# A TensorE-bound fused kernel on one core: a new plan with spare time at hand-overs, two groups normalised by VectorE from PSUM, and a new order of TensorE's steps

## The chip, the cores and the metric

The kernel runs on one core of one Trainium2 chip. The metric is the device time of one execution in microseconds. Before the change it took 386.89 us (median of three runs, 386.45 to 387.34).

## The reference

Two stages follow each other. The first is attention inside chunks of 64 rows, for 8 batches, 8 heads, 576 rows and a head size of 64. Its result, with the heads side by side, is the input x (8 x 576 x 512) of the second: four experts, each a causal attention with one head of 64, mixed by the softmax of the two largest of four gate logits.

```python
# stage 1, per batch, head and chunk of 64
scores = q_c @ k_c.T / sqrt(64); attn = softmax(scores); x = attn @ v_c
# stage 2, per batch and expert e
logits = x @ w_gate                     # two largest of four are kept
q, k, v = x @ wq[e], x @ wk[e], x @ wv[e]
a = softmax(causal(q @ k.T / sqrt(64)))
out += weight_e * (a @ v @ wo[e])       # weight_e: softmax over the two kept, else 0
```

## The kernel before, in words

Rows are cut into 36 groups of 128 (4608 rows in all). A unit is one or two groups; the first four units hold one group each. TensorE does its work in 374 named steps, and the letters name what a step does:

- `as` (line 532): score products of a unit's chunks, 64x64 matmuls in a quarter of the array. `as0.1` is half of `as0`; only units 0 and 1 (`FAST`) are split so.
- `at` (line 600): transposes of the normalised chunk weights, on half of the array's rows. `av` (line 621): their products with v, in quarters again; they give x.
- `m` and `v` (line 483): the projections of x to queries and keys (`m`, 52 steps of 12 matmuls) and to values and gate logits (`v`, 36 steps), on the full array. x and the weights are held as a high and a low part, and three products are added up. The first of these steps are split in two (`m1`, `m1.1`), so that the part that needs only high parts can go early.
- `s` (line 760): causal scores of an expert pair, six pieces for each of 16 pairs, on half of the rows. `st` (line 834): transposes of the finished weights. `o` (line 867): weights times values, on half of the columns, 16 steps. `w` (line 902): the output projection, 36 steps on the full array.

So a step has one of four forms of the array: full, rows (half of the rows), quarters, cols (half of the columns).

Between these, VectorE takes row maxima and subtracts them (lines 550, 562), sums exponentials (570, 575, 577), takes reciprocals (579), splits off low parts (644, 682, 684, 886), adds the causal mask and takes the minimum (772), and copies a part of the transposes and outputs (605, 814, 916). ScalarE takes exponentials (568, 573, 779) and copies from PSUM (464, 512, 608, 642, 677, 848, 882, 913). GpSimd multiplies the chunk weights by the reciprocals (586), makes the low parts of the weights (468), computes the gates (710 to 734) and scales the expert weights (803). Group 1 alone has its exponentials in PSUM (`FROM_PSUM`) and is normalised by VectorE (582), in two instructions.

There are eight PSUM banks, and they go round: a step takes the banks that were given back first. Which bank a step writes, and so whose copy it has to wait for, is fixed when the program is built.

The order is set in three ways. `ORDER` is a list, written out, of TensorE's steps. Every other queue (VectorE, ScalarE, GpSimd, SP with its transfers) is filled by a planner, `Plan.emit`, that runs through the program with a table of durations and delays and puts next, on each engine, the ready operation with the smallest key; the key is worked out backwards from the step of TensorE that needs the result (`rank`), and moved by tables (`LATER` by kind, `MOVED` by single operation, `EARLY` and `LOADS` for the first ones). `lat` is the delay that the planner puts between an operation and the one that uses its result. So the tables move instructions, while no duration in them is the chip's. Dummy matmuls (line 944, `FILLS`) stand at four places of the start.

## Time and profile before

| what | value |
|---|---|
| median of three runs | 386.89 us |
| the profiled execution | 386.81 us |
| its span, first to last instruction | 385.1 us |
| mean granted TensorE clock | 0.998 |
| TensorE matmuls busy | 376.4 us, 98% of the span |
| VectorE, ScalarE, GpSimd busy | 71%, 70%, 44% |
| moved by DMA | 40.76 MB, mean 106 GB/s |

The profiled execution took 1.7 us more than its span. In a timeline row the first two figures are the start and the length in us; then follow engine, source line, operation, destination and sources with shapes, and the count of merged instructions; in square brackets stands the idle time of the engine ahead of it and what ended that. A row of waits gives the waiting engine with its line, what it waited for, the total in us, the number of times and the longest. A matmul counts as busy until its modelled end, and the next one starts before that end, so busy time is not the sum of useful work. PEld is the loading of the stationary operand, which runs ahead of its matmul.

### The profile page before, as it was taken

The numbers are of one execution on the slowest core, as the hardware profiler recorded it, in microseconds if no ns is written. First come the engines' busy times: TensorE is split into PE (matmuls) and PEld (weight loads), VectorE is DVE, ScalarE is ACT, GpSimd is POOL, SyncE is SP. The second block draws the span as 40 slices with busy tenths as digits, with TensorE's granted clock in tenths as the row PEclk, the third lists the DMA queues.
The fourth block names the chain that finished last, engine by engine and source line by source line (L and its number), as shares of the span: only waits on it lengthen the run. The fifth ranks groups of instructions, "written<-read, shape, count | busy, mean of one in ns | idle before, by whom it ended". The sixth has DMA issues, their size and how long they took to land.

```text
span 385.1 us, 14193 instructions
## 1 busy us (share of the span) xinstructions
PE 376.4 (98%) x5604; PEld 331.7 (86%) x5605; DVE 272.4 (71%) x955; ACT 270.6 (70%) x899; POOL 170.4 (44%) x337
## 2 busy tenths in 40 slices
PE   7899999999999999999999999999999999999996
PEld 5699999978899979987999879988899998796764
DVE  3768989998984866968897375468739584557821
ACT  4565879797583995589935698349974597689551
POOL 7643167916354008950943002960651108624800
PEclk9999999999999999999999999999999999999999
DMA  7965726047450026420651200111101000000314
GB/s 270 383 213 180 219 86 220 5 129 243 162 184 2 4 91 233 174 83 3 228 183 59 84 0 30 48 63 47 69 34 53 0 24 35 2 30 0 139 56 163
DMA packets 22098, 40.76 MB, mean 106 GB/s; under 512 B 2448, under 2 KB 2704, under 8 KB 22032
## 3 DMA queue, kind: packets, MB, share of 16 engines
q1 hardware_dynamic: 21744, 39.47, 30.0%
q8 instruction: 44, 0.72, 0.8%
q10 hardware_dynamic: 288, 0.39, 0.3%
q14 instruction: 22, 0.18, 0.1%
HBM read 30.42 MB, written 9.44 MB: 104 GB/s over the span
## 4 chain that ended last, share of the span: by engine, by line
PE 88%; DVE 5%; ACT 4%; DMA 1%; issue 0%; SPq 0%; ACTq 0%; DVEq 0%
PE bank L483 39%; PE bank L902 12%; PE bank L760 10%; PE bank L867 10%; PE bank L834 6%; PE bank L621 4%; PE bank L532 4%; PE bank L600 2%; DMA qs<-in_qt_dram 1%; ACT at L779 1%; DVE mx L575 1%; DVE mx L550 1%; ACT aT L848 1%; DVE e L562 1%; ACT xh L642 1%; DVE aT L814 1%
## 5 line engine op out<-in xcount | busy, mean ns | idle before, releaser
L803 POOL TENSOR_SCALAR at<-at,st,gate 128x320 f32<-128x320 f32 (+4 forms) x160 | 94.5, 605 | 29.4 <-ACT at L779 16.2
L779 ACT ACTIVATE at<-at,st 128x320 f32<-128x320 f32 (+4 forms) x160 | 90.3, 598 | 0.9 <-DVE st L772 0.9
L483 PE MATMUL bank<-xh,wqk_hi 128*128 128x384 f32 (+1 forms) x208 | 66.1, 327 | 0.1
L483 PE MATMUL bank<-xl,wqk_hi 128*128 128x384 f32 (+1 forms) x208 | 65.1, 323 | 0.0
L483 PE MATMUL bank<-xh,wqk_lo 128*128 128x384 f32 (+1 forms) x208 | 65.1, 323 | 0.0
L848 ACT ACTIVATE aT<-bank 128x128 f32<-128x128 f32 (+2 forms) x256 | 57.6, 406 | 8.2 <-PE bank L834 8.1
L772 DVE CUSTOM_DVE_ANT_0 at<-bank,mask 64x64 f32<-64x64 f32 (+4 forms) x160 | 59.3, 423 | 3.4 <-PE bank L760 1.8
L586 POOL TENSOR_TENSOR e<-e,mx 128x1024 f32<-128x1024 f32 (+1 forms) x21 | 34.1, 1629 | 53.1 <-DVE mx L579 52.4
L867 PE MATMUL bank<-aT,vv 128*64 128x448 f32 (+4 forms) x384 | 45.0, 390 | 0.0
L867 PEld LDWEIGHTS bank<-aT,vv 128*64 128x64 f32 x384 | 24.4, 137 | 20.8 <-issue 15.4
L710 POOL TENSOR_TENSOR gs<-vv,gs 128x20 f32<-128x20 f32 x8 | 2.4, 299 | 89.5 <-DVE gs L704 89.5
L814 DVE STREAM_TRANSPOSE aT<-at 32x96 f32<-32x96 f32 x128 | 34.4, 269 | 9.7 <-POOL at L803 5.9
L483 PE MATMUL bank<-wvg_hi,xh 128*128 128x260 f32 x144 | 40.5, 288 | 0.0
L483 PE MATMUL bank<-wvg_lo,xh 128*128 128x260 f32 x144 | 39.8, 283 | 0.0
L483 PE MATMUL bank<-wvg_hi,xl 128*128 128x260 f32 x144 | 39.5, 281 | 0.0
L483 PEld LDWEIGHTS bank<-xh,wqk_hi 128*128 128x128 f32 x208 | 38.4, 188 | 1.0 <-ACT xh L642 0.2
L483 PEld LDWEIGHTS bank<-xl,wqk_hi 128*128 128x128 f32 x208 | 38.4, 189 | 0.2
L483 PEld LDWEIGHTS bank<-xh,wqk_lo 128*128 128x128 f32 x208 | 38.4, 188 | 0.0
L760 PE MATMUL bank<-kh,qh 64*128 64x288 f32 (+4 forms) x192 | 38.3, 338 | 0.0
L779 ACT ACTIVATION_READ_ACCUMULATOR at<-at,st 128x1 f32 (+1 forms) x160 | 37.6, 236 | 0.0
L760 PE MATMUL bank<-kl,qh 64*128 64x288 f32 (+4 forms) x192 | 34.3, 296 | 0.0
L760 PE MATMUL bank<-kh,ql 64*128 64x288 f32 (+4 forms) x192 | 32.8, 291 | 0.0
(96 smaller groups left out, 846.0 us busy)
## 6 DMA issues: line engine op xcount, KB each, us to landing
ks<-in_kt_dram SPq DMA_DIRECT2D x36, 256.0 KB, 4.6
vs<-in_vt_dram SPq DMA_DIRECT2D x36, 256.0 KB, 4.5
qs<-in_qt_dram SPq DMA_DIRECT2D x35, 256.0 KB, 4.7
out_dram<-y SPq DMA_DIRECT2D x35, 256.0 KB, 2.0
at<-in_wqk_dram SPq DMA_DIRECT2D x4, 256.0 KB, 5.7
at<-in_wvg_dram SPq DMA_DIRECT2D x2, 260.0 KB, 5.3
at<-in_wo_dram SPq DMA_DIRECT2D x2, 256.0 KB, 5.3
qs<-in_qt_dram ACTq DMA_DIRECT2D x1, 256.0 KB, 3.7
```

The lines of the kernel that those rows point to most:

```text
L483: pe.matmul(bk.t[:, :n_], a, x, start=(n == 0), stop=(n == 3 * KT - 1))
L532: pe.matmul(bq[s].t[cs, c0:c0 + 64], qs[n].t[own, hp, cs], ks[n].t[own, hp, cs], start=(n == 0 and hp == 0), stop=True, skip_group_check=True)
L586: od = [add("Pool", 0.14 + 0.87 * G, lambda: pool.tensor_tensor(e.t[:, al], e.t[:, al], mx.t[:, 3, al, 0:1].to_broadcast([128, 2 * nh, 64] ...
L760: pe.matmul(bks[s].t[:m, :w], q[own, cs], k[own, z0 + ks.start:z0 + ks.stop], start=(x == 0), stop=(x == 2))
L772: dve.tensor_tensor_reduce(out=a.t[:r, o_ + ks.start:o_ + ks.stop], in0=bk.t[:r, :w], in1=mask[:r, m0:m0 + w], scale=1.0, scalar=first, op ...
L779: act.activation(af, af, AF.Exp, scale=-1.0, bias=st.t[:r, 0, i, 0:1], accum_out=st.t[:r, 1, i, 0:1])
L803: pool.tensor_scalar(af, af, st.t[:r, 2, i, 0:1], gt.t[:r, i, e:e + 1], op0=OP.mult, op1=OP.mult)
L814: dve.transpose(dst, src)
L834: pe.transpose(bks[r].t[:, 64 * n:64 * n + 64], a.t[own, c0:c0 + 128], ident[own, own])
L848: act.activation(dst, bks[r].t[:, n:n + 64 * m].rearrange("p (j c) -> p j c", j=m), AF.Copy)
L867: pe.matmul(bk.t[64 * s:64 * s + 64, c0 - h0:h1 - h0], vs.t[:, j, 64 * (2 * pair + s):64 * (2 * pair + s) + 64], ts[s].t[:, place(s, j, c0 ...
L902: pe.matmul(bk.t, up[:, k, u0:u0 + 128], wp[:, k, :], start=(n == 0), stop=(n == 5))
```

## The change

It edits the planner's rules and its tables; the arithmetic changes at one place, group 0.

```diff
-FROM_PSUM = (1,)
+FROM_PSUM = (0, 1)
...
+SPARE = 0.07
+PAUSES = ((3.8, 0.4), (9.0, 1.3))
...
     def lat(self, a, b):
         if b.eng == "dma":
             return 1.9
+        if a.eng == "dma":
+            return 1.1 if b.eng == "ACT" else 0.8
         if a.eng == "SP":
             return 0.1
-        if a.eng == "dma":
-            return 0.9 if b.eng == "ACT" else 0.6
-        return self.LAT.get((a.eng, b.eng), 0.21)
+        return self.LAT.get((a.eng, b.eng), 0.21) + (SPARE if a.eng != b.eng else 0.0)
...
-        state = {"form": "full", "at": 192, "cross": 0.0, "block": 0.0, "pause": 1.2}
+        state = {"form": "full", "at": 192, "cross": 0.0, "block": 0.0}
...
+        pauses = list(PAUSES)
...
-                if eng == "dma" and now > 7.0 and state["pause"]:
-                    dur += state["pause"]
-                    state["pause"] = 0.0
+                if eng == "dma" and pauses and now > pauses[0][0]:
+                    dur += pauses.pop(0)[1]
...
-as0.1 as0 as1 as1.1 at0 at1 av0 av1 as2 m0 v0 v0.1 m2 as3 m1 v1 m1.1 m0.1 v1.1 m2.1 m3 m3.1 at2 at3 as4 av2 av3 as5
+as0.1 as0 as1.1 as1 at0 at1 av0 av1 as3 as2 m1 m0 m1.1 m3 m2 m3.1 m2.1 v1 m0.1 v0 as4 at3 at2 s0.1 s0 as5 av3 av2
...
-COLD = 6.5
+COLD = 8.0
...
-LOADS = [(x[:2], int(x[2:])) for x in "lq0 lq1 lv0 lv1 lw4 lw5 lw0 lw2 lw1 lw3 lq2 lv2 lq3 lv3 lq4 lv4".split()]
+LOADS = [(x[:2], int(x[2:])) for x in "lq0 lw4 lq1 lw5 lw0 lv0 lv1 lw2 lw1 lw3 lq2 lq3 lv2 lv3 lq4 lv4".split()]
```

`SPARE` and `PAUSES` are no instructions: they widen the delays with which the planner reckons, between two different engines by 0.07, and put two pauses into its picture of the transfers. `LATER`, `MOVED` and `EARLY` are replaced as well (`ap0@Pool` is gone from `EARLY`, `ap0` and `ap0.1` of VectorE are in it). All steps of `ORDER` are the same, in another sequence. Group 0's product with the reciprocals goes from one instruction of GpSimd (line 586) to two of VectorE (line 582 before, 586 after); its exponentials now go to PSUM. Lines of the changed kernel stand four further down.

Three places, as they stand in the program. First VectorE's queue from the second half of group 0's maxima on. `mx_84` belongs to group 0, `mx_85` to group 1. Before:

```order
L562 TENSOR_TENSOR e_81<-bank_62,mx_84 128x256 [waits DVE_49]
L570 TENSOR_REDUCE mx_84<-e_81 128x4 [waits Activation_49]
L550 TENSOR_REDUCE mx_85<-bank_64 128x4 [waits PE_49]
L570 TENSOR_REDUCE mx_84<-e_81 128x4 [waits Activation_49]
...
L579 RECIPROCAL mx_84<-mx_84 128x8 [waits DVE_49]
...
L579 RECIPROCAL mx_85<-mx_85 128x8 [waits DVE_49]
L582 TENSOR_TENSOR e_82<-bank_63,mx_85 128x256 [waits DVE_49]
L582 TENSOR_TENSOR e_82<-bank_64,mx_85 128x256
L605 COPY e_81<-bank_66 128x256 [waits PE_49]
L605 COPY e_82<-bank_68 128x256 [waits PE_49]
```

After:

```order
L566 TENSOR_TENSOR e_81<-bank_62,mx_84 128x256 [waits DVE_49]
L574 TENSOR_REDUCE mx_84<-bank_61 128x4 [waits Activation_49]
L554 TENSOR_REDUCE mx_85<-bank_63 128x4 [waits PE_49]
L554 TENSOR_REDUCE mx_85<-bank_64 128x4 [waits PE_49]
...
L583 RECIPROCAL mx_84<-mx_84 128x8 [waits DVE_49]
L586 TENSOR_TENSOR e_81<-bank_62,mx_84 128x256 [waits DVE_49]
L586 TENSOR_TENSOR e_81<-bank_61,mx_84 128x256
L574 TENSOR_REDUCE mx_85<-bank_64 128x4 [waits Activation_49]
...
L586 TENSOR_TENSOR e_82<-bank_63,mx_85 128x256 [waits DVE_49]
L609 COPY e_81<-bank_66 128x256 [waits PE_49]
L586 TENSOR_TENSOR e_82<-bank_64,mx_85 128x256
```

Group 0's two products now stand ahead of the last sum of group 1, and the copy of group 0's transposes stands between the two products of group 1.

Second, SP's queue of transfers at the start (q of group 0 goes through ScalarE's queue in both). Before:

```order
L425 DMA ks_73<-in_kt_dram 128x512
L461 DMA at_100<-in_wqk_dram 128x512
L425 DMA ks_74<-in_kt_dram 128x512
L426 DMA qs_70<-in_qt_dram 128x512
L461 DMA at_101<-in_wvg_dram 128x520 x2
L429 DMA vs_77<-in_vt_dram 128x512
```

After:

```order
L429 DMA ks_73<-in_kt_dram 128x512
L429 DMA ks_74<-in_kt_dram 128x512
L430 DMA qs_70<-in_qt_dram 128x512
L433 DMA vs_77<-in_vt_dram 128x512
L465 DMA at_100<-in_wqk_dram 128x512
L429 DMA ks_75<-in_kt_dram 128x512
```

k and q of group 1 (`ks_74`, `qs_70`) stand one place further up, ahead of the first piece of weights, and both pieces of the value weights (`wvg`) come later.

Third, TensorE's queue where the chunk weights of units 2 and 3 are transposed. A rank of eight transposes goes in turn to two banks; one row for each bank is shown. Before (`at2`, `at3`, `as4`, `av2`):

```order
L600 MATMUL bank_68<-ident,e_83 128x64 [waits Activation_49,Pool_49]
L600 MATMUL bank_63<-ident,e_83 128x64 [waits DVE_49]
...
L600 MATMUL bank_62<-ident,e_81 128x64 [waits Pool_49]
L600 MATMUL bank_64<-ident,e_81 128x64 [waits DVE_49]
...
L532 MATMUL bank_67<-ks_73,qs_69 64x64 [waits DMAHW3_49,DMAHW2_49,DVE_49]
...
L621 MATMUL bank_61<-e_83,vs_79 64x64 [waits DMAHW6_49,DVE_49,Activation_49]
```

After (`at3`, `at2`, `s0.1`):

```order
L604 MATMUL bank_62<-ident,e_81 128x64 [waits Pool_49]
L604 MATMUL bank_65<-ident,e_81 128x64 [waits DVE_49]
...
L604 MATMUL bank_63<-ident,e_83 128x64 [waits Pool_49]
L604 MATMUL bank_61<-ident,e_83 128x64 [waits DVE_49]
...
L764 MATMUL bank_62<-kh_94,qh_90 128x192 [waits Activation_49]
L764 MATMUL bank_65<-kh_94,qh_90 128x192 [waits Activation_49]
```

The two banks of `at3` are now written again by `s0.1`, with only the eight transposes of `at2` in between.

More of the change, by code (lines that the diff above doesn't have):

```diff
@@ L298 @@
-av17 av18 o8 o9 m42 v28 at19 s11.5 st43 s11 s11.2 s11.1 st42 st40 w19 v29 v27 v30 w20 m43 m41 av19 av20 as21 m40 m45
-m44 m47 m46 st44 st46 s12.2 st45 s12.4 st47 s12.5 st41 s12.1 s13.4 s12 at21 s13.5 s13.1 s13.2 s13.3 s12.3 s13 av21
-w21 v31 m49 m51 w18 m50 m48 o11 o10 st50 st51 st55 st49 v32 v34 v33 w23 v35 st48 s14.4 st52 st53 s14.1 s14 s15.4 s15
-st54 s14.5 s15.2 s15.1 s15.5 s14.3 s14.2 s15.3 o13 o12 w24 w25 w22 w26 st60 st58 st61 st63 w28 w27 w29 st62 st59
-st56 st57 o15 o14 w30 w33 w34 w35 w31 w32
+as0.1 as0 as1.1 as1 at0 at1 av0 av1 as3 as2 m1 m0 m1.1 m3 m2 m3.1 m2.1 v1 m0.1 v0 as4 at3 at2 s0.1 s0 as5 av3 av2
@@ new lines @@
+v0.1 v1.1 as6 m7 v2 m5 v3 s1 at4 at5 s1.2 s1.3 m6 as8 av5 av4 as7 m4 m10 m8 v4 m11 m9 s0.3 at6 s1.4 s0.2 s0.4 av6
+s1.1 at7 s1.5 s0.5 as10 av7 as12 v8 m12 v5 v7 m13 m14 st6 st5 at8 st1 st4 m15 v6 st0 st7 s3.1 s3.3 st2 st3 s2.2 s2.5
+s2.4 as9 av8 o1 o0 s3 s2 s2.3 at12 at10 s3.4 s3.5 s2.1 s3.2 at9 v10 m18 v9 v11 m19 as11 av9 as13 av10 m16 m17 m20
+m22 v12 m23 st8 st9 st12 m21 st10 st11 s4.4 st14 s4.1 at11 s4 st13 s4.5 s5.1 at13 s4.2 st15 s5.4 s5.5 s4.3 s5.2 s5.3
+av11 as16 o3 o2 w1 v13 v17 w0 w2 m24 v16 w4 v14 w6 st17 s5 st16 av12 av13 as15 as14 w7 m25 v15 m27 m26 w5 st20 st19
@@ new lines @@
+st21 w3 w8 st22 s7.4 st18 s7.1 at16 s6 st23 s7.2 at14 s6.2 at15 s6.4 s6.1 s6.5 s7.5 s7.3 s6.3 o4 o5 s7 st27 st25
+av14 as18 av15 w11 m29 v21 v19 m33 m28 w9 st24 st28 m30 m31 v20 v18 m32 m35 st30 s8.2 st26 st31 s9.1 s9 st29 s9.2
+s9.3 s9.5 s9.4 o6 o7 as19 av16 as20 w10 v22 m34 m37 v23 v25 w12 m39 s8 at19 s8.4 st38 at18 s8.1 s8.3 s8.5 at20 av18
+as17 w13 w16 v24 m38 v26 m36 w14 w15 st34 st36 s11.3 st37 s11.4 st35 s11.1 st33 s11.5 st39 s11.2 at17 s10.3 st32
+s10.2 s10.1 s10.4 av19 av17 o8 o9 s11 s10.5 s10 m41 v27 m42 v28 v30 st46 st45 st41 st42 as21 av20 m40 m46 m47 v29
@@ L303 @@
+m45 m43 m44 st40 st44 s12.2 st47 s13.4 st43 s13.1 s13.5 s12 at21 s12.4 s12.1 s12.5 s13 s13.3 s12.3 s13.2 av21 o11
+o10 v31 m49 w18 w20 w19 w17 m48 w21 w22 st55 st54 st49 m51 v33 m50 v34 st50 s15.2 st48 st51 s15.4 s15.3 s15 v32 w23
+v35 s14 st52 s15.1 st53 s14.4 s14.1 s14.2 s14.3 s14.5 s15.5 o13 o12 w25 w24 w26 st58 st59 st57 st63 st56 w27 w29 w28
+st62 st60 st61 o14 o15 w30 w33 w32 w35 w31 w34
 """
 LATER = {
-    "lw@SP": -42.42, "wh@ACT": 29.36, "wl@Pool": 185.94, "lq@SP": 58.01, "lv@SP": -84.07, "ad@DVE": 77.63,
@@ L306 @@
-    "aa@ACT": -67.07, "ap@Pool": 29.29, "ac@ACT": -300.91, "ac@DVE": 37.56, "ax@ACT": -85.88, "ay@DVE": -86.29,
-    "ap@DVE": 59.59, "za@ACT": -311.41, "zd@DVE": 141.75, "va@ACT": -94.8, "g@DVE": 55.2, "g@Pool": -72.89,
-    "g@ACT": 126.17, "sd@DVE": -10.35, "sa@ACT": 247.27, "sp@Pool": -67.79, "sc@ACT": 8.88, "sx@DVE": 189.81,
-    "oa@ACT": 55.54, "od@DVE": -167.08, "y@DVE": 72.2, "so@SP": 224.14, "y@ACT": -191.59, "so@ACT": 160.08}
-MOVED = {
[28 rows of a table removed]
-COLD = 6.5
+    "lw@SP": -132.04, "wh@ACT": 47.15, "wl@Pool": 166.02, "lq@SP": 19.61, "lv@SP": -136.46, "ad@DVE": 113.5,
@@ L341 @@
+    "aa@ACT": -157.54, "ap@DVE": 117.39, "ac@ACT": -289.24, "ac@DVE": -30.41, "ax@ACT": -216.87, "ay@DVE":
+    -146.29, "ap@Pool": 5.46, "za@ACT": -322.71, "zd@DVE": 240.29, "va@ACT": -119.4, "g@DVE": 30.75, "g@Pool":
+    -112.84, "g@ACT": 186.21, "sd@DVE": -75.67, "sa@ACT": 235.31, "sp@Pool": -41.46, "sc@ACT": -74.3, "sx@DVE":
+    283.68, "oa@ACT": 40.3, "od@DVE": -142.3, "y@DVE": 100.98, "so@SP": 292.84, "y@ACT": -197.53, "so@ACT":
+    165.02}
+MOVED = {
[30 rows of a table added]
+COLD = 8.0
 FILLS = {("as", 1): 2, ("at", 0): 7, ("av", 0): 2, ("at", 1): 2}
@@ L343 @@
 TURNS = (0.246, 0.423)
-LOADS = [(x[:2], int(x[2:])) for x in "lq0 lq1 lv0 lv1 lw4 lw5 lw0 lw2 lw1 lw3 lq2 lv2 lq3 lv3 lq4 lv4".split()]
-EARLY = [x + "@DVE" for x in ("ad0 ad0.1 ad0.2 ad0.3 ad0.4 ad0.5 ad0.6 ad0.7 ad1 ad1.1 ad1.2 ad1.3 ac0 ad1.4 ad1.5 ay0 ay0.1 ad1.6 "
-                              "ad1.7 ap1 ap1.1 ac1 ay1 ay1.1").split()]
-EARLY += ["ap0@Pool"]
+LOADS = [(x[:2], int(x[2:])) for x in "lq0 lw4 lq1 lw5 lw0 lv0 lv1 lw2 lw1 lw3 lq2 lq3 lv2 lv3 lq4 lv4".split()]
+EARLY = [x + "@DVE" for x in ("ad0 ad0.1 ad0.2 ad0.3 ad0.4 ad0.5 ad0.6 ad0.7 ap0 ap0.1 ad1 ad1.1 ad1.2 ad1.3 ac0 ad1.4 ad1.5 "
+                              "ad1.6 ad1.7 ap1 ap1.1 ay0 ay0.1 ac1 ay1 ay1.1").split()]
 EARLY += [x + "@ACT" for x in "aa0 aa0.1 aa1 aa1.1 wh4 ac0 ax0 ax0.1 wh5 ac1 ax1 ax1.1 wh0 wh2 wh1 wh3".split()]
```

9 lines of the change are left out of this document (removed), and 58 rows, old and new, of the table MOVED.

## The prediction

> **What bounds the kernel now.** I read the page first: its span, the busy time of the engines, and then busy time by stretch.
>
> ```profile
> span 385.1 us, 14193 instructions
> PE 376.4 (98%) x5604; PEld 331.7 (86%) x5605; DVE 272.4 (71%) x955; ACT 270.6 (70%) x899; POOL 170.4 (44%) x337
> ```
> ```profile
> 0.00:14.00 14.00, 9.71 (x190) 6.88 (x195) 6.79 (x21) 6.80 (x13) 10.85 (x41) 1.00 0.87 307
> 14.00:381.00 367.00, 366.22 (x5427) 324.85 (x5420) 265.65 (x934) 263.21 (x885) 159.59 (x297) 1.00 0.29 98
> 381.00:385.10 4.10, 0.45 (x2) 0.01 (x1) 0.00 (x0) 0.60 (x1) 0.00 (x0) 0.82 0.34 128
> ```
>
> The columns behind the length are TensorE's matmuls, its weight loads, VectorE, ScalarE and GpSimd. From 14 to 381 us TensorE is busy for 366.22 of 367.00 us, so in that stretch only TensorE's own work, and waits short enough to hide behind the draining of a matmul, can be gained or lost. The last 4.1 us (copy and store of the last output tile) are untouched: `w32` before and `w34` after are both tiles that ScalarE copies. What is left is the start. The hidden waits show in the weight loads. The view of waits of PEld from 14 to 382 us, without its rows on "issue", has 13 waits for other engines, 4.2 us together; the three longest kinds and the last:
>
> ```profile
> PEld bank L834 <- DVE y L916: 0.9, 1, 0.9
> PEld bank L760 <- ACT aT L848: 0.5, 2, 0.4
> PEld bank L867 <- DVE st L772: 0.5, 2, 0.3
> ...
> PEld bank L600 <- ACT aT L848: 0.2, 1, 0.2
> ```
> ```profile
> PE bank L834 <- DVE y L916: 0.6, 1, 0.6
> ```
>
> The second fence is the same view for the matmuls: of the 0.9 us that the load waited, 0.6 were lost to them, and no other wait is seen there. A load runs ahead of its matmul, so a load's wait overstates the loss.
>
> **The start.** First TensorE, then VectorE, then one row of GpSimd, in the timeline.
>
> ```profile
> 4.57 1.03 PE L532 MATMUL bank<-ks,qs 64*64 64x64 f32 x32 [0.18 <-DMA qs<-in_qt_dram]
> 7.37 0.98 PE L532 MATMUL bank<-ks,qs 64*64 64x64 f32 x32 [1.22 <-DMA qs<-in_qt_dram]
> 11.17 0.47 PE L600 MATMUL bank<-ident,e 64*128 64x64 f32 x8 [1.21 <-POOL e L586]
> 12.54 0.47 PE L600 MATMUL bank<-ident,e 64*128 64x64 f32 x8
> 12.94 0.60 PE L944 MATMUL bank<-y 128*128 128x512 bf16 x2
> 13.47 1.16 PE L621 MATMUL bank<-e,vs 64*64 64x64 f32 x64
> ```
> ```profile
> 5.82 0.42 DVE L562 TENSOR_TENSOR e<-bank,mx 128x256 f32<-128x256 f32 x1
> 6.16 0.41 DVE L550 TENSOR_REDUCE mx<-bank 128x4 f32<-128x256 f32 x1
> 6.61 0.42 DVE L562 TENSOR_TENSOR e<-bank,mx 128x256 f32<-128x256 f32 x1
> 6.95 0.41 DVE L570 TENSOR_REDUCE mx<-e 128x4 f32<-128x256 f32 x1
> 8.39 0.42 DVE L550 TENSOR_REDUCE mx<-bank 128x4 f32<-128x256 f32 x1 [1.03 <-PE bank L532]
> ...
> 11.52 0.20 DVE L579 RECIPROCAL mx<-mx 128x8 f32<-128x8 f32 x1
> 11.76 0.76 DVE L582 TENSOR_TENSOR e<-bank,mx 128x256 f32<-128x256 f32 x2
> ```
> ```profile
> 10.07 1.05 POOL L586 TENSOR_TENSOR e<-e,mx 128x512 f32<-128x512 f32 x1 [0.18 <-DVE mx L579]
> ```
>
> Group 0's transposes (11.17) waited for GpSimd, group 1's (12.54) for VectorE, which had stood idle for 1.03 us because group 1's scores came late (7.37).
>
> **The change part by part.**
>
> *Loads.* Group 1's k and q are ahead of a 256 KB piece of weights now. That piece was in ScalarE's hands at 5.64 and group 1's q came 1.7 us later, two transfers on:
>
> ```profile
> 5.64 0.63 ACT L464 ACTIVATE wqk_hi<-at 128x512 fp32r<-128x512 f32 x1 [2.92 <-DMA at<-in_wqk_dram]
> ```
>
> So a transfer is worth about 0.85 us, group 1's scores come at about 6.5, and the 1.03 us of idle time go.
>
> *Group 0 by VectorE.* From the rows, an independent instruction of 256 columns starts 0.34 us behind the one before it (5.82 to 6.16), a dependent one 0.45 (6.16 to 6.61), and a product 0.24 behind its reciprocal (11.52 to 11.76). The new queue by hand: sum at 6.95; maxima of group 1 at 7.29 and 7.63; subtraction 7.97; second sum of group 0 8.31; subtraction 8.65; small sum 8.99; first sum of group 1 9.06; reciprocal 9.40; two products, 9.64 and 9.98, done at 10.40. Group 0's transposes then go at 10.45, not 11.17: 0.7 us won, as GpSimd's 1.05 us give way to 0.76 us. But VectorE goes on in one queue: sum 10.32, small sum 10.77, reciprocal 10.95, product 11.19, copy of group 0's transposes 11.53, second product 11.87, done at 12.28. Group 1's transposes go at 12.33, 0.2 us earlier, and `av0`, the two dummies and all that follows stand behind them. I take -0.2. The ends: -0.7, the gain of group 0 alone, if the rest follows it; and +0.6, one weight copy of ScalarE (0.63) that stands ahead of group 1's exponentials and waits for its transfer.
>
> *Form changes.* Two rows each of the same work, from the chain of waits:
>
> ```profile
> 165.00 1.40 PE bank L902 x6
> ...
> 168.32 1.59 PE bank L902 x6
> ```
> ```profile
> 184.61 1.87 PE bank L532 x128
> ...
> 195.87 2.02 PE bank L621 x128
> ```
>
> An output projection between two full-array steps takes 1.40 us, a lone one between transposes and scores 1.59. 128 quarter matmuls followed by other half-array work take 1.87 us, followed by full-array work 2.02. Into the full form and out again thus costs 0.15 + 0.19 = 0.34 us. Counted over the two lists without the dummies, form changes go from 66 to 74: into the full form 24 to 25, out of it 23 to 24, among the three small forms 19 to 25. One pair costs 0.34; no row prices the six small ones, so between 0 and the 0.17 of half a pair I take 0.1, nearer to the pair. That is +0.94, with ends 0.3 and 1.4. [...]
>
> *Waits later on.* The 4.2 us of load waits, less 0.1 us each that the load ran ahead, are a loss of 2.9 us; the ends are 0.6 (what the matmuls show) and 4.2. The planner now keeps 0.07 us at each hand-over, and the two programs show it where TensorE goes back to a bank: reckoned with the pace of the steps, 63 of the 368 steps before write a bank within 1.0 us of its last writer, 53 after; within 0.8 us 20 and 15. The shortest cover from a unit's transposes to their products (units 2 on) rises from 0.9 to 1.5 us, that from `st` to `o` from 1.2 to 2.9. I let 0.6 of the 2.9 us stay: -2.3, and for the ends +0.3 (the visible 0.6 goes, 0.9 us of new ones come) and -3.5.
>
> *One new wait.* `s0.1` writes the banks of `at3` behind only the eight transposes of `at2`, 0.25 us. ScalarE must copy both first, and does such copies four in a row:
>
> ```profile
> 25.48 1.21 ACT L608 ACTIVATE e<-bank 128x256 f32<-128x256 f32 x4
> ```
>
> 0.30 us for the first, 0.39 till the second is done, and some 0.1 to hand over: 0.8 less 0.25 of cover is +0.5, between 0.3 and, behind a weight copy, 0.9. Behind it in TensorE's queue stand `s0`, `as5` and the rest, so it counts in full.
>
> *At nothing.* The new orders of loads and stores: the DMA share is 0.29 from 14 to 381 us, and no load of TensorE waits for a transfer there; uncovered, one late group would cost about the 0.85 us of a transfer. GpSimd's lost 1.05 us are off the path behind 14 us (44% busy).
>
> The sum: -0.2 + 0.94 - 2.3 + 0.5 = -1.06 on the profiled execution's 386.81 (span 385.1 and 1.7 around it, left as it is). That execution lies 0.08 below the median of 386.89, so 385.8 is my forecast in terms of the median. A change of 0.2% (0.77 us) is about what a measurement of this kernel can tell from none.
>
> **The rivals.**
>
> *The waits were never a loss.* TensorE at 366.22 of 367.00 us, and 0.6 us of matmul waits, say that only 0.6 can be won there. Then -0.2 + 0.94 - 0.6 + 0.5 = +0.64: 387.5, no change that can be told. Against it: short waits inside the drain of a matmul would not be seen as idle time.
>
> *The start gives all.* If group 0's 0.7 us carry through and all 2.9 us of waits go, with 0.6 for the form changes and 0.3 for the new wait, the sum is -2.7: 384.2. For it speaks that GpSimd and the late load were what released TensorE there; against it that VectorE has to do both groups.
>
> *The end is bound by GpSimd* (slower). The last 20 scalings need the gates of the last batch, which need a reciprocal of VectorE behind a queue of score minima. Before:
>
> ```profile
> 345.35 0.24 POOL L726 TENSOR_SCALAR gs<-gs 128x5 f32<-128x5 f32 x1
> 351.59 0.23 POOL L731 TENSOR_TENSOR gs<-gs 128x20 f32<-128x20 f32 x1 [6.00 <-DVE gs L728]
> ...
> 352.54 10.23 POOL L803 TENSOR_SCALAR at<-at,st,gate 128x320 f32<-128x320 f32 x17
> ```
>
> The scalings began at 352.54, 11.6 us behind the last values' projection (`v35`, whose copies ran from 340.95):
>
> ```profile
> 340.95 0.78 ACT L512 ACTIVATE vv<-bank 64x260 f32<-64x260 f32 x2 [0.84 <-PE bank L483]
> ```
>
> Each takes 0.60 us (10.23 / 17). After, the first transposes that need them (`st58`) come about 14.5 us behind `v35`, where before it was 19, and the first five steps follow in 1.5 us. If the gap stays 11.6 us, the 12 scalings that these five steps need are done 11.6 + 12 x 0.60 = 18.8 us behind `v35`, when TensorE wants the last of them at 16: +2.8 us, and with the rest of the sum 388.6. It decides from a gap of about 8.8 us on, each further us costing one. Against it: fewer minima stand ahead of the reciprocal (33 rows of VectorE's queue between the gate's first instruction and it, 52 before), so I expect some 8.5 us, just short of that point.
>
> **How the numbers follow.** My forecast has 0.40: 385.8, of which two thirds fall below the 386.1 that counts as faster and a third between. The start that gives all has 0.20, all faster. The waits that were no loss have 0.20: 0.16 the same, 0.04 slower. GpSimd at the end has 0.20: 0.01 the same, 0.19 slower. Faster 0.27 + 0.20 = 0.47; same 0.13 + 0.16 + 0.01 = 0.30; slower 0.04 + 0.19 = 0.23. The range goes from just under the second rival, 384.1, to 388.2, where the end would cost 2.4 of its 2.8 us; half of the last rival and a little at the bottom stay out, under 2 in 10. Cases of both signs hold the chance; the forecast's own range, with the ends of its terms taken one at a time, is 384.6 to 387.0.
>
> **What would show it.** Right: group 0's transposes at about 10.5 and no row of GpSimd at line 590 ahead of them; group 1's at about 12.3, the first value products at 13.3; a wait of half a us of the scores (L764) for ScalarE (L612) about 10 us later; load waits from 14 us on well under 4.2 us; a lone output projection still 1.59. Wrong: load waits of 4 us or more, a GpSimd that scales without a pause while the last transposes wait, or group 1's transposes later than 12.54, which would make the start a loss.

## The result and the profile after

The changed kernel took 389.71 us (median of five runs, 388.76 to 390.64), beside 386.89 for the kernel before (five runs, 386.45 to 387.46). The ratio is 1.0067, with an interval from 1.0047 to 1.0088. The forecast of 385.8 was wrong in sign, and the time lies above the range. The profiled execution is the one of 388.76 us, the shortest of the five; its span is 387.0 us, against 385.1 before.

The head of its page, and busy time by stretch (columns as in the prediction):

```profile
span 387.0 us, 14185 instructions
PE 379.4 (98%) x5605; PEld 332.7 (86%) x5605; DVE 270.7 (70%) x957; ACT 270.6 (70%) x899; POOL 169.0 (44%) x336
```
```profile
0.00:14.00 14.00, 11.48 (x157) 7.75 (x157) 7.24 (x23) 4.83 (x10) 6.22 (x38) 1.00 0.87 299
14.00:383.00 369.00, 367.48 (x5449) 324.98 (x5448) 263.42 (x935) 265.21 (x889) 162.75 (x299) 1.00 0.29 98
383.00:387.00 4.00, 0.43 (x2) 0.00 (x0) 0.00 (x0) 0.60 (x1) 0.00 (x0) 0.83 0.35 131
```

The tail is as it was. TensorE, though, is busy for 11.48 us of the first 14, where it was 9.71. It has no more work there, so it does that work more slowly. Its timeline from 4 to 16 us shows where:

```profile
4.43 1.61 PE L536 MATMUL bank<-ks,qs 64*64 64x64 f32 x32
5.97 1.04 PE L948 MATMUL bank<-y 128*128 128x512 bf16 x2
6.94 1.61 PE L536 MATMUL bank<-ks,qs 64*64 64x64 f32 x32
8.49 2.49 PE L948 MATMUL bank<-y 128*128 128x512 bf16 x7
11.14 0.58 PE L604 MATMUL bank<-ident,e 64*128 64x64 f32 x8 [0.16 <-DVE e L586]
...
13.34 0.46 PE L604 MATMUL bank<-ident,e 64*128 64x64 f32 x8 [1.08 <-DVE e L586]
...
14.27 1.16 PE L625 MATMUL bank<-e,vs 64*64 64x64 f32 x64
```

The 32 score products took 1.03 and 0.98 us in the profile of before and take 1.61 here. This execution began at half TensorE's pace, though the column of the granted clock says 1.00 throughout. The column is blind there: the trace's list of clock changes opens with a rise to the full clock, at 10.16 us here and at 4.73 in the profile of before, and the time ahead of its first entry counts as 1.00. VectorE's rows show the effect: it got through group 0's first half and then stood idle for 0.51 us (before: 1.03), because group 1's scores were not ready.

```profile
7.18 0.42 DVE L574 TENSOR_REDUCE mx<-bank 128x4 f32<-128x256 f32 x1
8.11 0.92 DVE L554 TENSOR_REDUCE mx<-bank 128x4 f32<-128x256 f32 x2 [0.51 <-PE bank L536]
```

So the first value products (L625) start at 14.27, where before had 13.47 and I expected 13.3. That is 0.8 of the 1.9 us between the two spans. Most of the rest is a stall further on. The waits of TensorE's matmuls from 14 to 384 us, and the place of the longer one in its timeline:

```profile
PE bank L536 <- issue: 0.9, 1, 0.9
PE bank L764 <- ACT e L612: 0.3, 1, 0.3
```
```profile
30.09 1.04 PE L536 MATMUL bank<-ks,qs 64*64 64x64 f32 x55
32.00 0.38 PE L536 MATMUL bank<-ks,qs 64*64 64x64 f32 x9 [0.87 <-issue]
```

The scores of unit 6 (`as6`) stop after 55 of 64 products for 0.87 us and wait for nothing that the profile shows ("issue"). The other wait is the one foreseen for the banks of `at3`. The load waits behind 14 us, without their rows on issue, fell only from 4.2 us (13 waits) to 3.8 (14); the longest kinds now:

```profile
PEld bank L838 <- POOL at L807: 0.6, 2, 0.4
PEld bank L871 <- DVE st L776: 0.5, 2, 0.3
PEld bank L625 <- DVE st L776: 0.5, 2, 0.3
PEld bank L764 <- ACT e L612: 0.4, 1, 0.4
```

A simple split serves for what follows: the start is the time to the first L621/L625 product, the rest runs from there to the end of the span. Before: 13.47 + 371.6. After: 14.27 + 372.7, of which 0.9 is the stall; without it 371.9 are left, still no less than before.

### The profile page after: what moved, and what is told of

The parts are those of the page before. It is cut to its first block, busy times and chain, and to the rows that moved or that the text cites. A ratio compares the mean times of both kernels' runs of the same rounds, so it can differ in the third digit from the quotient of the medians.

```text
span 387.0 us, 14185 instructions
## 1 busy us (share of the span) xinstructions
PE 379.4 (98%) x5605; PEld 332.7 (86%) x5605; DVE 270.7 (70%) x957; ACT 270.6 (70%) x899; POOL 169.0 (44%) x336
## 4 chain that ended last, share of the span: by engine, by line
PE 94%; ACT 2%; DVE 1%; issue 1%; POOL 1%; DVEq 0%; POOLq 0%; ACTq 0%
PE bank L487 40%; PE bank L906 13%; PE bank L764 11%; PE bank L871 10%; PE bank L838 6%; PE bank L536 5%; PE bank L625 5%; PE bank L604 2%; ACT at L783 1%; PE bank L944 1%; POOL at L807 1%; ACT e L612 0%; DVE e L586 0%; PE bank L948 0%; DVE mx L574 0%
## 5 line engine op out<-in xcount | busy, mean ns | idle before, releaser
L807 POOL TENSOR_SCALAR at<-at,st,gate 128x576 f32<-128x576 f32 (+4 forms) x160 | 94.4, 602 | 44.8 <-ACT at L783 24.1
L783 ACT ACTIVATE at<-at,st 128x192 f32<-128x192 f32 (+4 forms) x160 | 89.8, 589 | 0.1
L776 DVE CUSTOM_DVE_ANT_0 at<-bank,mask 128x320 f32<-128x320 f32 (+4 forms) x160 | 59.5, 424 | 18.6 <-PE bank L764 17.0
L590 POOL TENSOR_TENSOR e<-e,mx 128x1024 f32<-128x1024 f32 (+1 forms) x20 | 33.0, 1656 | 51.2 <-DVE mx L583 42.8
L783 ACT ACTIVATION_READ_ACCUMULATOR at<-at,st 128x1 f32 (+1 forms) x160 | 36.3, 227 | 0.0
L516 ACT ACTIVATE vv<-bank 64x260 f32<-64x260 f32 (+1 forms) x56 | 21.5, 383 | 17.1 <-PE bank L487 16.5
```

The source lines that it names most:

```text
L516: act.activation(v_s[b].t[p0:p0 + m, j], bk.t[r0:r0 + m, 0:W_VG], AF.Copy)
L590: od = [add("Pool", 0.14 + 0.87 * G, lambda: pool.tensor_tensor(e.t[:, al], e.t[:, al], mx.t[:, 3, al, 0:1].to_broadcast([128, 2 * nh, 64] ...
L776: dve.tensor_tensor_reduce(out=a.t[:r, o_ + ks.start:o_ + ks.stop], in0=bk.t[:r, :w], in1=mask[:r, m0:m0 + w], scale=1.0, scalar=first, op ...
L783: act.activation(af, af, AF.Exp, scale=-1.0, bias=st.t[:r, 0, i, 0:1], accum_out=st.t[:r, 1, i, 0:1])
L807: pool.tensor_scalar(af, af, st.t[:r, 2, i, 0:1], gt.t[:r, i, e:e + 1], op0=OP.mult, op1=OP.mult)
```

## The experiments

Eighteen experiments ran, in five groups; each group shared a chip with runs of before.

**1 and 2. Both kernels again.** No edit.

> The kernel before, once more, for its start. Theory A (TensorE's clock at the start is a matter of chance): the first score products of 16 matmuls take 0.4 us or 0.7 us, not always the same as in the other profile of this kernel (0.4), and the dummies 0.22 or 0.42 us. Theory B (the change makes TensorE's start slow): always 0.4 and 0.22 us, the first value products at 13.5 us.

> The changed kernel, once more. Theory A: the 16 matmuls of a half score product take 0.7 us in one profile and 0.4 in another, and the first value products come at 13.3 to 14.3 us accordingly. Theory B: again 0.7 us, dummies of 0.42 us until 10 us, value products at 14.3. The gap of 0.9 to 1.0 us inside as6 near 31 us: there again if it is the fetching of instructions behind the transfers (theory F), gone if it was an accident of one run.

Measured: 387.83 us (span 386.1) for before, 387.19 (span 385.5) for the changed kernel, one execution each; before's median on this chip was 387.43 (23 runs). This time before began at half pace too. Its TensorE at the start:

```profile
4.53 1.61 PE L532 MATMUL bank<-ks,qs 64*64 64x64 f32 x32
...
7.26 1.61 PE L532 MATMUL bank<-ks,qs 64*64 64x64 f32 x32 [0.15 <-DMA qs<-in_qt_dram]
8.81 3.17 PE L944 MATMUL bank<-y 128*128 128x512 bf16 x7
11.91 0.69 PE L600 MATMUL bank<-ident,e 64*128 64x64 f32 x8
...
14.48 1.16 PE L621 MATMUL bank<-e,vs 64*64 64x64 f32 x64
```

and the one row that answers in the changed kernel:

```profile
14.35 1.16 PE L625 MATMUL bank<-e,vs 64*64 64x64 f32 x64
```

The pace of the start is thus not fixed by the program: before starts its value products at 13.47 or at 14.48 us. That is theory A for before; the changed kernel began at half pace in both its profiles. Half-pace start against half-pace start the change wins 0.13 here, but its three such profiles (14.27, 14.35, and 14.67 in experiment 6) lie on both sides of before's one at 14.48, so a gain of 0.2 is not shown. There was no stall in `as6` this time, and the rest took 371.15 us against before's 371.6. The whole profiled loss of 1.9 us is gone between these two executions, but the median of the first five runs is not explained by that.

**3. The scores of unit 6 two steps later.**

```diff
-v0.1 v1.1 as6 m7 v2 m5 v3 s1 at4 ...
+v0.1 v1.1 m7 v2 m5 as6 v3 s1 at4 ...
```

> The changed kernel with the step as6 (64 small matmuls, 128 instructions) behind m7, v2 and m5 rather than ahead of them. Theory F (TensorE ran out of fetched instructions in as6, as 256 of them went by in under 5 us while the fetch took 1.9 us behind loads): the gap near 31 us goes, and the time falls by about 1.0 us to 388.7. Rival (the scores waited for a bank or for their loads and the wait only shows late): the gap moves with as6, and the time stays at 389.7.

Measured: 387.90 us, ratio to before 1.0017 (1.0002 to 1.0032); no stall in `as6`. The stall did not move with `as6`, as theory F wants it, but experiment 2 had none at the old place either, so this profile alone does not decide. It shows something else, which set the course of the later experiments. TensorE was at full pace by 6 us, did the seven dummies in 1.68 us, and then had little to do:

```profile
7.52 1.68 PE L948 MATMUL bank<-y 128*128 128x512 bf16 x7
10.68 0.58 PE L604 MATMUL bank<-ident,e 64*128 64x64 f32 x8 [1.48 <-DVE e L586]
11.19 0.39 PE L948 MATMUL bank<-y 128*128 128x512 bf16 x1
12.88 0.69 PE L604 MATMUL bank<-ident,e 64*128 64x64 f32 x8 [1.30 <-DVE e L586]
13.50 1.03 PE L948 MATMUL bank<-y 128*128 128x512 bf16 x2
14.47 1.84 PE L625 MATMUL bank<-e,vs 64*64 64x64 f32 x64
```
```profile
9.20:12.60 3.40, 0.90 (x10) 0.55 (x10) 3.19 (x13) 1.50 (x5) 1.33 (x2) 1.00 1.05 399
12.60:16.00 3.40, 3.12 (x66) 2.17 (x70) 0.65 (x2) 1.86 (x5) 3.40 (x3) 0.50 1.06 389
```

The second fence is busy time by stretch of the same kernel; the column behind GpSimd is the granted clock. After 3.4 us in which TensorE was busy for 0.90 its clock was halved, for 3.4 us (the clock entries stand at 12.60 and 16.02). The gaps around it were of 1.48 and 1.30 us, the second still open when the clock fell. So it fell behind a stretch in which TensorE was merely little busy.

**4. Group 0 by VectorE, on the kernel before, alone.**

```diff
-FROM_PSUM = (1,)
+FROM_PSUM = (0, 1)
-EARLY = [x + "@DVE" for x in ("ad0 ... ad0.7 ad1 ...
+EARLY = [x + "@DVE" for x in ("ad0 ... ad0.7 ap0 ap0.1 ad1 ...
-EARLY += ["ap0@Pool"]
```

> The kernel before with one part of the change: group 0 normalised by VectorE from PSUM, all tables and the order of TensorE's steps as before. If this part moves the start as reckoned with all loads as before (group 0's transposes earlier by up to 0.5 us, group 1's later, since VectorE's queue has two more instructions of 0.34 us each): 386.9 to 387.6. If it is the source of the loss: 388.5 or more.

Measured: 388.44 us, ratio 1.0029 (1.0016 to 1.0041). TensorE in its profile:

```profile
10.77 0.58 PE L599 MATMUL bank<-ident,e 64*128 64x64 f32 x8 [0.86 <-DVE e L581]
...
12.84 0.67 PE L599 MATMUL bank<-ident,e 64*128 64x64 f32 x8 [1.17 <-DVE e L581]
...
13.97 1.16 PE L620 MATMUL bank<-e,vs 64*64 64x64 f32 x64
```

Group 0's transposes come 0.4 us earlier than before (11.17), group 1's 0.3 later (12.54), the value products 0.5 later. So this edit is a loss at that place: the time that GpSimd worked beside VectorE now stands in VectorE's one queue, ahead of group 1. The median, 1.0 above before, all but reaches the 388.5 that I had set for the source of the loss, and no run of it has a low clock (0.995 or more); 0.5 of that is seen here, the other half is not located.

**5 to 8. The changed kernel timed, and three single parts**, all on one chip, where before took 387.70 us (23 runs).

Number 6, the changed kernel as it is, no edit:

> The changed kernel as it is, timed on the chip of the next three. Theory A (the loss is the sum of places in the program, with the 0.9 us stall inside as6 coming in some executions and not in others): the median lies 1 to 2.5 us above before, and the runs of this kernel spread over 1.5 us or more; where the profile has no stall inside as6, its span is within 1 us of before's. Theory B (the loss was a cold start by chance): the median is within 0.5 us of before.

Measured: 388.71 us (387.26 to 390.08, 12 runs), ratio 1.0030 (1.0014 to 1.0047). Each run lists its mean granted clock, and the runs fall in two groups by it: five at 0.999 to 1.000 took 387.26 to 388.25 (mean 387.6), seven at 0.990 to 0.994 took 388.60 to 390.08 (mean 389.4). Seven of twelve at 1.8 us more is 1.0 us, all of the difference of the medians, and before's fourteen runs at 0.999 or more took 387.6 us as well. Theory A holds by its numbers (the median, and a spread of 2.8 us), but what parts the runs is the clock, which it did not name. Of the first five runs of the changed kernel three had 0.990. The counts below draw the line at 0.991. That is what 6.8 us at half clock, two windows, make of this span (experiments 5 and 10); one window gave 0.996 in experiment 3, so a shorter loss is not counted, and a half clock in the tail, as in before from 383.6 us on, lowers the mean too.

Number 5, the score pieces of `s0` behind `as5`:

```diff
-... m0.1 v0 as4 at3 at2 s0.1 s0 as5 av3 av2
+... m0.1 v0 as4 at3 at2 as5 s0.1 s0 av3 av2
```

> The changed kernel with the score pieces s0.1 and s0 behind as5 in place of ahead of it, so that as5 (about 1 us of quarter matmuls) covers the two copies of ScalarE whose banks s0.1 writes. Theory A (the wait for those banks costs 0.6 us at this place): the wait of L764 for L612 near 26 us goes, and the median is 0.4 to 0.6 us under that of the changed kernel beside it (one change of form more or less moves that by 0.1 to 0.2). Theory B (the wait is hidden by another limit right behind it): the same time within 0.2 us, with a new wait ahead of av2 or av3.

Measured: 390.36 us (six runs), ratio 1.0071 (1.0048 to 1.0095). Theory A falls. Of theory B the new wait ahead of the value products came, but the time did not stay: the wait went elsewhere and grew, and half of the runs had a low clock. The matmuls' waits, and busy time by stretch at the start:

```profile
PE bank L625 <- DVE st L776: 0.8, 1, 0.8
PE bank L536 <- ACT e L612: 0.3, 1, 0.3
```
```profile
7.50:10.90 3.40, 1.08 (x5) 0.29 (x3) 2.28 (x9) 1.21 (x3) 1.00 (x1) 0.99 1.05 388
10.90:14.30 3.40, 2.16 (x18) 1.33 (x20) 2.41 (x9) 1.60 (x4) 1.63 (x3) 0.50 1.05 365
14.30:17.70 3.40, 3.40 (x102) 2.71 (x104) 1.31 (x4) 2.08 (x7) 2.37 (x2) 0.50 1.05 389
```

This execution, too, began at full pace and lost its clock, here for two windows: it fell behind 1.08 of 3.40 us busy, stayed down behind 2.16 of 3.40, and rose behind a full 3.40. TensorE stood idle for 2.62 us ahead of group 0's transposes, and only a part of that is due to the early scores. The rest is ScalarE: its weight copy stands ahead of group 1's exponentials and waits for its transfer, and VectorE waits behind it.

```profile
9.12 0.63 ACT L468 ACTIVATE wqk_hi<-at 128x512 fp32r<-128x512 f32 x1 [1.72 <-DMA at<-in_wqk_dram]
```
```profile
10.06 0.42 DVE L574 TENSOR_REDUCE mx<-bank 128x4 f32<-128x256 f32 x1 [1.08 <-ACT bank L572]
```

That is the end of +0.6 that the prediction gave the start: the weights whose place in the queue of transfers went to group 1's k and q now come late.

Number 7, group 0 on GpSimd again, within the changed kernel:

```diff
-FROM_PSUM = (0, 1)
+FROM_PSUM = (1,)
-    "ap0@DVE": 0.29, "ap0.1@DVE": 3.43,
+    "ap0@Pool": -0.2,
```

> The changed kernel with group 0 normalised by one instruction of GpSimd again, all else kept. Theory A (VectorE's one queue is the loss at the start, 1.0 us as in the reverse experiment on before): group 0's transposes come some 0.4 to 0.7 us later, group 1's some 0.5 to 1 us earlier, the first value products 0.5 to 1 us earlier, the median 0.5 to 1 us under the changed kernel. Theory B (TensorE's clock at the start sets it, not the engine): the first value products within 0.2 us where the paces of the score products agree, and the same median within 0.3 us. Theory C (the prediction: group 0 by VectorE wins): the median is 0.2 us or more above the changed kernel.

Measured: 388.72 us, ratio 1.0030 (1.0013 to 1.0048), the same as the changed kernel, with five of twelve clocks at 0.991 or less. Theory B for the median. In its profile (a start at half pace) the value products stand at 13.89, earlier than the changed kernel's three (14.27, 14.35, 14.67), so the loss of experiment 4 is there, but it is not what makes the median.

Number 8, the planner's rules alone, on before:

```diff
+SPARE = 0.07
+PAUSES = ((3.8, 0.4), (9.0, 1.3))
-COLD = 6.5
+COLD = 8.0
```

with the lines on `lat` and pauses as in the change.

> The kernel before with the planner's new rules alone (0.07 us more at each hand-over, the two pauses, the later warm clock), its order of TensorE's steps, its tables and group 0 on GpSimd kept. Theory A (the waits saved come with the new order of steps and the tables, the rules by themselves move other engines' instructions without aim): within 0.7 us of before, to either side, with waits of the weight loads of 3.5 us or more behind 14 us. Theory B (the spare time by itself takes the waits away, as the prediction had it): load waits under 3 us and 1 us or more faster than before.

Measured: 390.60 us, ratio 1.0071 (1.0058 to 1.0084). Neither theory: I had allowed 0.7 us, it lost 2.9. The load waits without issue are 5.5 us (17), more than before's 4.2; the longest of the matmuls:

```profile
PE bank L836 <- DVE y L918: 0.5, 1, 0.5
PE bank L836 <- DVE kl L686: 0.5, 1, 0.5
```

More time at each hand-over in the planner's picture took no wait away here by itself; the three edits ran together, and which of them cost the 2.9 us is not known.

**9 to 12. The clock.** The theory by then: group 1's scores come so early that a TensorE at full pace runs out of work ahead of group 0's transposes and loses its clock. One weight piece ahead of group 1's k and q again (the first edit; it is a piece of the value weights, where before has one of the weights of q and k); the dummies of before taken away (the second, on before); the changed kernel's seven dummies spread, two more added ahead of group 1's transposes, and three tiny matmuls that wait for VectorE in between (the third); the third together with experiment 3's edit.

```diff
-    "lw4@SP": 102.66,
+    "lw4@SP": 0.0,
```
```diff
-FILLS = {("as", 1): 2, ("at", 0): 7, ("av", 0): 2, ("at", 1): 2}
+FILLS = {("as", 1): 2, ("at", 0): 0, ("av", 0): 2, ("at", 1): 2}
```
```diff
-FILLS = {("as", 1): 2, ("at", 0): 7, ("av", 0): 2, ("at", 1): 2}
+FILLS = {("as", 1): 2, ("at", 0): 9, ("av", 0): 2, ("at", 1): 5}
+GATES = {("at", 0, 6): "ad1.1@DVE", ("at", 0, 3): "ad1.3@DVE", ("at", 1, 3): "ad1.7@DVE"}
...
+            pe.matmul(banks[-1][:, 0:t.shape[1]], ident, t, start=True, stop=True)
```

> The changed kernel with one 266 KB piece of weights ahead of group 1's k and q again, as before. Clock theory (group 1's scores come so early that TensorE, when it starts at full pace, stands idle for 2.6 us ahead of group 0's transposes, and its clock then halves for some 3.4 to 7 us; that is the loss): group 1's scores start at 7.2 or later, mean granted clocks of 0.991 or less in at most 2 of 12 runs (in 20 of 47 runs of the changed kernel and its variants so far, in 1 of 46 of before), the median 0.8 to 1.2 us below the changed kernel, which lay 1.0 above before. Rival (the loss lies behind the start: form changes, banks, the stall inside as6): the median stays 0.8 to 1.2 us above before.

> The kernel before without the seven dummy matmuls ahead of group 0's transposes, so that TensorE stands idle from about 8.4 to 11.2 us there too. Clock theory: mean granted clocks of 0.991 or less in a third of the runs or more, and those runs 1.5 to 2.5 us longer than the others; the median 0.8 us or more above before. Rival (idle time at the start is free, the clock falls by chance): clocks as before, and the same median within 0.3 us.

> The changed kernel with its seven dummies ahead of group 0's transposes spread out (two of the places wait for a subtraction of VectorE), and two more ahead of group 1's, behind its reciprocal; every other engine's queue is word for word the same. Clock theory: no idle stretch of TensorE over 1.3 us at the start, clocks of 0.991 or less in at most 2 of 12 runs, the median 0.8 to 1.2 us below the changed kernel, so level with before or up to 0.3 us under it; executions that start at full pace come out near 386. Rival (the loss lies behind the start): the median stays 0.8 to 1.2 us above before.

> The same with the scores of unit 6 two steps later as well, where no stall was seen inside them. If clock and stall together are the loss, the median lies 0.3 to 1.0 us below before. If the spread dummies do not hold the clock, it stays 0.5 us above, as with the later scores alone.

| kernel | median us | ratio to before (387.43) | clocks of 0.991 or less |
|---|---|---|---|
| group 1 late | 387.88 | 1.0011 (0.9998 to 1.0023) | 0 of 12 |
| before, no dummies there | 387.93 | 1.0016 (1.0002 to 1.0030) | 9 of 12 |
| dummies spread | 387.83 | 1.0016 (1.0002 to 1.0029) | 0 of 12 |
| dummies spread, `as6` later | 388.00 | 1.0023 (1.0010 to 1.0036) | 0 of 12 |

The counts settle from both sides what the gap does to the mean clock. Take the gap away and no run is low; make the gap in the kernel before and nine of twelve are. The stretch ahead of group 0's transposes in three kernels, in this order: before, before without dummies (two windows, as its clock entries bound them), the spread dummies:

```profile
8.35:11.75 3.40, 2.19 (x16) 0.96 (x17) 3.07 (x11) 1.59 (x5) 2.98 (x3) 1.00 1.04 393
```
```profile
4.32:7.73 3.41, 1.99 (x61) 1.61 (x62) 1.93 (x5) 1.38 (x4) 2.53 (x13) 1.00 0.94 321
7.73:11.14 3.41, 0.58 (x17) 0.40 (x10) 2.69 (x9) 2.02 (x4) 2.42 (x3) 0.50 1.07 408
```
```profile
9.20:12.60 3.40, 2.99 (x20) 1.42 (x19) 3.19 (x12) 1.38 (x4) 1.27 (x1) 1.00 1.05 394
```

The middle fence corrects the picture, though. In this execution the clock fell at 7.73, ahead of the place of the missing dummies (8.3 in before), behind a window with 1.99 us of matmuls; before kept its clock through one with 2.04 (4.73 to 8.15). What went with the gap here was a second window at half clock, until 14.56.

In time the theory was half right. I expected 0.8 to 1.2 us less than the changed kernel, level with before; the changed kernel stood 1.0 above before (on the chip of experiment 6; it did not run on this one), these two 0.4, and their intervals overlap with its. Moving `as6` as well gave nothing: 388.00 after 387.83. In the kernel before the missing dummies cost 0.5 us, not 0.8, and its four runs at 0.991 took 387.6 us in the mean, 0.2 above before's median; the five at 0.986 or 0.987 took 388.8. So a low mean clock has no fixed price; that it depends on what TensorE had to do in those microseconds is my guess and was not tested. The spread dummies also cost where the start is slow, since each takes 0.43 us there: the value products of that profile stand at 14.73.

**13 to 16. Order and start apart; a longer warm-up.** The new order with nearly the old start (experiments 7 and 9 together; the transfers behind that one piece keep their new order); the same with `as6` later; that with 72 in place of 64 small matmuls at the very start; and the latter on before.

```diff
-    for _ in range(64 if banks else 0):
+    for _ in range(72 if banks else 0):
```

> The new order and tables with the old start: group 0 normalised by GpSimd, and a weight piece ahead of group 1's k and q. Theory S (the start is the loss, order and tables behind it are worth the 0.9 us that the prediction summed up for them): the median is 0.4 to 0.9 us below before, no mean clock of 0.991 or less in more than 2 of 12 runs. Theory O (the order itself gives nothing, its form changes and its bank wait eat what it saves): within 0.3 us of before. The prediction's rival that the waits were never a loss: 0.5 us or more above before.

> The same with the scores of unit 6 two steps later. If the stall inside them comes in many executions, the median falls by a further 0.3 to 0.8 us and the scatter shrinks; if it is rare, the same within 0.2 us.

> The same again with 72 in place of 64 small matmuls at the very start, so that TensorE is busy until group 0's q has come (4.4 to 4.8 us) and does not fall idle ahead of the first scores. If a start at half pace (dummies 0.43 us apart until about 10 to 13 us, where others have 0.22) is set by such gaps, more executions start at full pace and the median falls by 0.3 to 0.7 us; if it is chance, the same within 0.2 us.

> The kernel before with the 72 small matmuls alone. By the same theory the median falls by 0.3 to 0.7 us; if the pace at the start is chance, the same within 0.2 us.

Measured, beside 387.61 for before: 388.89, ratio 1.0025 (1.0012 to 1.0038); 387.90, 1.0009 (0.9994 to 1.0023); 388.25, 1.0019 (1.0008 to 1.0031); 387.22, 0.9993 (0.9981 to 1.0006). Theory S falls: with the old start and the clock held the new order does not win 0.4 us or more. Theory O holds for the second. The first, 1.28 above before, meets the condition of the third reading, that the waits were never a loss. Between the first two lies 1.0 us, and the first one's profile has the stall at the same place as the changed kernel's:

```profile
30.34 1.04 PE L537 MATMUL bank<-ks,qs 64*64 64x64 f32 x55
32.26 0.35 PE L537 MATMUL bank<-ks,qs 64*64 64x64 f32 x9 [0.88 <-issue]
```

The 1.0 us is not the price of the stall alone: the first one's profile also has a wait of 0.56 us for a transfer of q at 16.1 us, which the second one's lacks. The packed traces (all that the profiler kept of a run) fit theory F of experiments 2 and 3. They list the transfers of instructions, and one queue (`q8 instruction: 44, 0.72, 0.8%` on the pages of before and of the changed kernel) carries 44 of 16 KB. TensorE has 11,210 matmuls and loads, an estimated 255 for each; that these transfers are TensorE's is inferred from that count. In the two profiles with the stall the last one ahead of it ended at 30.59 and 30.71 us, only 0.3 and 0.5 us before the stop. In five of the six others with `as6` at this place the same one ended 1.3 us or more ahead of the 55th product; in the sixth, experiment 9, it ended 0.8 us ahead, and the products paused there for 0.5 us. No run changed the transfer alone.

The longer warm-up gives nothing that can be told from none (388.25 after 387.90 for the new order). In before's profile with it q of group 1 came late, TensorE stood idle for 2.05 us and did group 1's scores at half pace, since its clock was halved from 7.33 to 14.16 us:

```profile
8.05 1.61 PE L532 MATMUL bank<-ks,qs 64*64 64x64 f32 x32 [2.05 <-DMA qs<-in_qt_dram]
```

**17 and 18. That gap filled:** four dummies in place of two ahead of group 1's scores, on experiment 16 and on 15.

```diff
+            for _ in range(2 if n[0] < 3 else 1):
                 pe.matmul(banks[-1], warm[:, 0:128], warm, start=True, stop=True)
```

> The kernel before with 72 small matmuls at the very start and four dummies in place of two between the scores of group 0 and of group 1. Clock theory: mean clocks of 0.991 or less in no run, starts at full pace in most, the median 0.4 to 0.8 us below before. If two more dummies delay group 1's scores where the start is slow (each 0.43 us there), the two effects cancel and the median is within 0.3 us of before.

> The new order with the old start, the later scores of unit 6, 72 small matmuls and the same two more dummies. If the new order is worth its forecast once the start is held, the median is 0.5 to 1 us below before; if form changes and waits cancel, as the single profiles of the last batch say (waits behind 15 us 5.2 us in the mean, before 6.2, against 0.94 us of form changes), it is within 0.3 us of the kernel beside it.

Measured, beside 387.16: 387.41, ratio 1.0014 (1.0001 to 1.0026), and 388.40, 1.0029 (1.0014 to 1.0045). Both profiles start at full pace and keep it to the value products, which come at 13.21 and 13.38, among the earliest. For before it is worth nothing in the median. For the new order neither reading holds: with no low clock in twelve runs it is 1.24 above before. Its profile shows where a part went, all behind the start: 0.69 us for a transfer of q at 15.7 us, two stalls on issue of 0.60 and 0.56 (64.5 and 160.1 us, each 1.3 us behind the end of a transfer of instructions), and the 0.28 of the banks of `at3`. No version was found that beats the kernel before.

## Why the prediction was wrong

**The start (forecast -0.2, ends -0.7 and +0.6): this step failed.** Its rows came from an execution that began at full pace, and the queue by hand treated TensorE as an engine that only waits. The hand schedule itself was near in experiment 3: with TensorE at full pace by 6 us group 0's transposes came at 10.68 (expected 10.45), group 1's at 12.88 (12.33). But 12.88 lies beyond 12.54, the sign that I had set for a loss, and in experiment 5 they came at 11.20 and 13.40. What it left out is TensorE's clock. With the 1.03 us of idle time that I took from VectorE group 1's scores went forward, the seven dummies with them, and a stretch of 1.5 to 2.6 us without work opened in front of group 0's transposes, in experiment 5 in part by the weight copy that I had named as the bad end. In 20 of the 48 runs of kernels that have both the early scores and the dummies in a block the mean clock was 0.991 or less; in kernels without it (experiments 4, 8, 9, 11 to 14) in none of 77, in the four with the longer warm-up in 2 of 47, and in 1 of 139 of before on those chips. On experiment 6's chip the seven runs at 0.994 or less are the whole loss, so what I had put at -0.2 stood for +1.0 in the median there; where both kernels started at half pace the value products lay between 0.21 earlier and 0.19 later.

**Group 0 by VectorE** was a gain of 0.7 for group 0 in the working. Alone it gave 0.4 there and lost 0.5 at the value products, through group 1. Within the changed kernel it made no difference that the median shows (experiment 7).

**The new wait at `s0.1` (+0.5): right in place and size.** The row says 0.3 us for the matmuls; measured against the pace of the steps around it, `s0.1` and `s0` start 0.64 us late (0.45 and 0.19).

**Waits later on (-2.3) and form changes (+0.94): this step failed too.** From the first value products to the end of the span before took 371.6 us in both its profiles, and experiments 10, 16 and 17, which differ from it only ahead of that, 371.3 to 372.1. The changed kernel took 371.15 and 371.33 in its two profiles without the stall and 371.9 in the first one less its stall. That is -0.5 to +0.3 where the three terms together said -0.86, and within the scatter of before: a gain behind the start is not shown, and no timed run of the new order with the clock held lies below before. The size was wrong at the price of a load wait. I took off 0.1 us for each, while the one wait that both views show cost the load 0.9 and the matmuls 0.6; with 0.3 off each, the 13 waits come to an estimated 1.0 us, not 2.9. The load waits themselves fell by only 0.4. No run changed the form changes alone, so 0.94 remains an estimate, and how much of the waits went stays open. The mechanism that I named, the planner's 0.07 at each hand-over, did not show by itself in experiment 8. One sum is off as well: with +0.3 for the waits alone the forecast's own range ends at about 388.3, not at 387.0.

**The stall in `as6`: not in the sum at all.** It was 0.87 and 0.88 us in two profiles; in timed runs moving the step was worth 1.0 us between experiments 13 and 14 and nothing between 11 and 12. It comes and goes with the same program. That a block of instructions arrives late there fits the transfers of instructions beside experiment 13 (ended at 30.59 and 30.71 us), and was not tested by an edit.

**The rivals.** GpSimd at the end did not come to pass, though its 388.6 is nearest to the 389.71: TensorE's loads waited 0.36 us for its scalings at 361.8, its matmuls not visibly. That the waits were never a loss (387.5, +0.64) is nearest to the +1.0 of experiment 6, and no run contradicts its part behind the start; it left out the start. The rival that came true was not among mine: that a transfer which came earlier left the engine it feeds slower, as in experiments 3 and 5 (half clock from 12.60 and from 10.85 us).

What stays open: with the clock held (no low run, or one) the new order still lies 0.3 to 1.3 us above before in seven kernels (experiments 9, 11 to 15 and 18), and four of their intervals start at 1.0008 or higher; late transfers of q and of instructions are seen in single profiles and were not timed apart. On the first chip the loss was 2.8 us. Its three runs at a low clock lay 1.1 above its other two, which is 0.7 in the mean, and those two still lay 2.0 above before's mean; the stall accounts for 0.9 of that if it came in both.

## What to carry to other kernels

Before you bring work forward on an engine whose clock can fall, as TensorE's did here behind 0.90 us of matmuls in 3.40 (experiment 3), add up how long it will stand idle afterwards: here the wait removed at the front went with gaps of 1.48 and 2.62 us behind it (experiments 3 and 5). Profile the start of a kernel more than once, and list clocks beside times: the first two profiles here began at different paces, and neither showed the fall of the clock. A stall that the rows call issue came in one execution of the changed kernel (0.87 us) and not in the next, so one pair of runs does not price it; look at the transfers of instructions beside it.
